# Holding the loads of two thirds back behind one-element copies, and moving the row sums and scalings of a third, in an attention kernel with a low-rank token mixer and an MLP

## Chip, cores and metric

One core of a Trainium2 chip runs the kernel. The metric is the device time of one execution in microseconds (us). Each of the five engines works through its own queue of instructions in program order: TensorE (PE, matmul), VectorE (DVE), ScalarE (ACT), GpSimd (POOL) and SyncE (SP). SP and POOL also issue DMAs, each into a queue of its own; 16 DMA engines serve both queues.

## What is computed

Attention with RMS-normalised queries and keys, then a mixer over the tokens and an MLP over the channels. B = 8 batches, 12 heads, 448 tokens, head size 64, so 768 channels; rank 32; hidden size 3072.

```python
q_n, k_n = rmsnorm(q, g_q), rmsnorm(k, g_k)
attn = softmax(q_n @ k_n.T / 8)
x = (attn @ v)                                # as [batch, 448, 768]
u = x + ((x.transpose(0, 2, 1) @ U) @ V).transpose(0, 2, 1)
out = u + relu(u @ w_ch1) @ w_ch2
```

## The kernel before, in words

A *third* is four heads of one batch: thirds 0 to 2 are batch 0, thirds 3 to 5 batch 1. A *pair* is two heads: pairs 0 to 5 are batch 0, pair 6 begins batch 1. Of each third, SP loads k and q (`load`, L209; side 0 is k, side 1 is q) and v (`load_v`, L220), 448 KB each. POOL or ACT squares k and q (`squares`, L234 and L236), DVE sums the squares by row (`reduce`, L242), ACT makes the reciprocal roots with a logarithm and an exponential (`rsqrt`, L247 and L248), and DVE scales into the bf16 tile `qkn` of a pair (`scale`, L256). There are two such tiles, used in turn. TensorE transposes a pair (`turn`, L267), DVE copies the result (`keep`, L274 and L278), TensorE makes the scores (`scores`, L300), ACT takes the exponentials (`expo`, L305), TensorE weighs v (`weigh`, L326), and DVE divides by the sums (`normalise`, L336 and L343).

For batch 0 the mixer goes in steps of 128 channels, `dc` = 0 to 5: `gather(dc)` (L401) multiplies by U, `gathered` copies, `spread(dc)` (L415, L417) multiplies by V, and `spreaded` (L422, L424) copies into `us[0]`, the MLP's input. The hidden layer is made in 24 blocks of 128. For batch 0, `first(i, ...)` (L889) makes blocks 0 to 3 channel by channel, as the channels arrive; `mlp(0)` makes blocks 4 to 23 (L541), and ACT or DVE evacuates them (L544, L546). The first weight w1 is loaded by POOL in four pieces (`load_w1`, L184): columns 0 to 511, 512 to 1023, 1024 to 2047 and 2048 to 3071. In hidden blocks these are 0 to 3, 4 to 7, 8 to 15 and 16 to 23. The second weight w2 comes in six pieces (`load_w2`, L192), the first behind `load_w1(3)`.

The order of the beginning is written out by hand: `head()` (L666 to L877) loads thirds 0 to 3 and the mixer's U and V (`load_mix`, L154 and L155), then goes through a list `plan` of steps. The steps fill the engines' queues in that order. The loads of thirds 4 and 5 stand in the plan, so they are issued on SP as soon as SP comes to them and their buffers are free. After `head()`, `weave` puts pieces of batch 1's attention between the blocks of `mlp(0)`, at due times that follow from weights: first `transposes(6)` (`turn(6)` and `keep(6)`), `load_w2(0, 0)` and the row sum of third 4's k, then what `attention(1)` lists. There POOL squares third 4's q and third 5's k and q, and casts the values of thirds 4 and 5, with the later pieces of w2 between them in its queue.

Some storage is borrowed: thirds 2 and 3 are loaded into `hT`, the place of the hidden layer; the squares of thirds 0 to 3 lie in `w2b`, the place of w2. A one-element copy on POOL after each scaling of the other thirds (`yield_port`, L573) makes POOL wait until DVE has scaled.

Of the kernel before, what the change touches and what calls it, by code (L numbers as in the profile page):

```python
# [10 lines left out]
BF16 = mybir.dt.bfloat16  # L11
# [6 lines left out]
def kernel(  # L18
# [13 lines left out]
    nc = tc.nc  # L32
# [27 lines left out]
    consts = ctx.enter_context(tc.tile_pool(name="consts", bufs=1))  # L60
# [135 lines left out]
    qks, vts, sqs, rstds, qkns, qkTs, scs, pts = {}, {}, {}, {}, {}, {}, {}, {}  # L196
# [29 lines left out]
    ALL = slice(0, HG)  # L226
# [42 lines left out]
    def keep(p, s, eng=None):  # L269

        if p not in qkTs:
            qkTs[p] = attn.tile([P, 2, S], BF16, tag="qkT", name="qkT")
        if s:
            nc.vector.tensor_scalar(qkTs[p][:, 1], pts[p][:, 1], gg, None, OP.mult)  # L274
        elif eng:
            nc.scalar.activation(qkTs[p][:, 0], pts[p][:, 0], AF.Copy)
        else:
            nc.vector.tensor_copy(qkTs[p][:, 0], pts[p][:, 0])  # L278

    def transposes(p):  # L280
        if p < NPE:
            turn(p)
            keep(p, 1)
            keep(p, 0)
        else:
            qkTs[p] = attn.tile([P, 2, S], BF16, tag="qkT", name="qkT")
            nc.sync.dma_start_transpose(qkTs[p].rearrange("d s (j p) -> d (s j) p", j=NJ),
                                        qkns[p].rearrange("p s j h d -> p (s j) (h d)"))
# [377 lines left out]
    def head():  # L666
# [33 lines left out]
            (squares, 1, ALL, (0,)),  # L700
            (gain,),
            (keep, 0, 0, 1),
            (heat, 13),
            (yield_port, 0, 1),
# [29 lines left out]
            (expo, 1, 0),  # L734
            (scores, 1, (1,)),
            (scores, 1, (2,)),
            (load, 4),
            (turn, 3),
            (expo, 1, 1),
            (scores, 1, (3,)),  # L740
# [19 lines left out]
            (setup_u, 1),  # L760
            (setup_u, 2),
            (cast_v, 1),
            (load_v, 4),
            (expo, 2, 2),
            (keep, 3, 0),
            (weigh, 0, 1),
# [16 lines left out]
            (keep, 4, 0),  # L783
            (normalise, 1, 0),
            (keep, 4, 1),
            (load, 5),
            (scores, 3, (2,)),
            (weigh, 1, 1),
            (scores, 3, (3,)),
# [10 lines left out]
            (gathered, 1, 1),  # L800
            (gathered, 0, 1),
            (scores, 4, (1,)),
            (load_v, 5),
            (scores, 4, (2,)),
            (spread, 1),
            (scale, 2, 1, (1,)),
            (turn, 5),
            (load_w1, 1),
            (normalise, 2, 0),
# [33 lines left out]
            (scores, 5, (3,)),  # L843
            (spread, 3),
            (spreaded, 2),
            (reduce, 3),
            (gather, 4),
            (expo, 5, 2),
            (squares, 4, ALL, (0,)),
# [4 lines left out]
            (spreaded, 3, 1),  # L854
            (weigh, 5, 0),
            (first, 1, (0, 1, 2, 3), True),
            (rsqrt, 3),
            (normalise, 5, 1),
            (normalise, 5, 0),
            (gather, 5),  # L860
            (scale, 3, 0),
            (gathered, 4, 1),
            (gathered, 5, 1),
            (spread, 4),
            (first, 0, (3,), False),
            (spreaded, 4, 1),
            (spread, 5),
            (first, 0, (4,), False),
            (spreaded, 5, 1),
            (first, 1, (4,), False),  # L870
            (first, 0, (5,), False),
            (first, 1, (5,), False),
            (scale, 3, 1),
            (load_w1, 3),
        ]
        for fn, *args in plan:
# [44 lines left out]
    with tc.manual_schedule():  # L921
        head()
        late = {7: (load_w2s, 1, 3), 8: (load_w2s, 3, 5), 9: (load_w2s, 5, 6)}
        for b in range(B):
            fill, total = mlp(b), volume(b)
            if b + 1 < B:
                later = []
                rest = [(4, lambda: (load_w2(0, 0), transposes(6), reduce(4, ALL, (0,))))] + attention(1, late, later)
                weave(fill, total * (0.72 if b in (4, 6, ) else FA[b % 2] if b else FA0), attention(b + 1) if b else rest)
                weave(fill, total * FM, mixing(b + 1))  # L930
                if b == 0:
                    weave(fill, total * FL, [(5 if w == .5 else 1, piece) for w, piece in later])
            for _ in fill:
                pass
# [30 lines left out]
```

## Time and profile before

| | |
|---|---|
| median of 4 runs | 576.16 us (575.08 to 576.36) |
| the profiled execution | 576.36 us |
| its span, first to last instruction | 574.6 us |
| PE, DVE, ACT, POOL busy | 98%, 67%, 49%, 14% of the span |
| `gather(5)` starts | 39.35 us |
| hidden block 4 starts (`mlp(0)`) | 41.90 us |
| the scores of pair 6 start | 46.30 us |
| hidden block 8 starts | 49.09 us |
| scalings of third 3 | 39.21 to 43.79 us |
| third 4: k, q, v issued | 22.21, 24.91, 26.26 us |
| third 5: k, q, v issued | 29.12, 33.76, 39.40 us |
| third 5: k, q, v landed | 56.2, 60.5, 63.8 us |
| third piece of w1 issued, landed | 29.21, 49.05 us |

Times are microseconds from the start of the span. In a row of a timeline the first number is the start and the second the duration; the square bracket gives the idle time of the engine before it and what ended that. In the chain of work that ended last, each row is a start, a length and what took it. A table by stretches gives the busy time of each engine with its number of instructions, the granted share of TensorE's clock, the busy share of the DMA engines (two queues can overlap on an engine, so it can pass 1) and the rate in GB/s. A row of a DMA queue gives packets, MB and the share of the 16 engines' time.

### The profile page before, as it was taken

What the parts mean: (1) busy time and instruction counts of PE and PEld (TensorE: products, weight loads), DVE (VectorE), ACT (ScalarE), POOL (GpSimd) and SP (SyncE); (2) the same over time, 40 slices, a digit from 0 to 9 for tenths busy, and PEclk for the clock granted to TensorE, in tenths of its full rate; (3) what the DMA queues carried; (4) which work ended last, traced back from release to release, by engine and by line L of the source; (5) the groups of instructions that cost most, each with busy time, mean ns of one, the idle gap of its engine ahead of it and who ended that gap; (6) DMA issues with size and microseconds to landing.
All of it is one profiled execution on the core that took longest, in us unless ns stands there. A gap on an engine that the chain in (4) does not pass through costs nothing.

```text
span 574.6 us, 11397 instructions
## 1 busy us (share of the span) xinstructions
PE 561.4 (98%) x4661; PEld 311.6 (54%) x4661; DVE 385.4 (67%) x755; ACT 280.2 (49%) x419; POOL 78.6 (14%) x124
## 2 busy tenths in 40 slices
PE   7998999999999999999999999999999999999997
PEld 5664555544565555544465555644456555654464
DVE  5985865799875788647776588747767486443442
ACT  5965652466621875076631777146661476302200
POOL 5662500100020000001020010000011000000010
PEclk9998999999999999999999999999999999999999
DMA  9999995733444565435534446455334541140021
GB/s 215 239 240 233 211 163 148 160 97 65 128 120 106 128 127 144 91 91 114 129 83 109 106 129 142 119 119 129 85 77 126 124 98 33 30 110 2 0 56 55
DMA packets 103648, 67.22 MB, mean 117 GB/s; under 512 B 54716, under 2 KB 102060, under 8 KB 103596
## 3 DMA queue, kind: packets, MB, share of 16 engines
q1 hardware_dynamic: 93988, 56.77, 41.8%
q0 software_dynamic: 9376, 9.44, 9.9%
q8 instruction: 36, 0.59, 0.4%
q10 hardware_dynamic: 232, 0.30, 0.1%
q14 instruction: 16, 0.13, 0.1%
HBM read 52.19 MB, written 11.01 MB: 110 GB/s over the span
## 4 chain that ended last, share of the span: by engine, by line
PE 90%; DMA 4%; DVE 2%; ACT 2%; POOL 1%; issue 0%; DVEq 0%; POOLq 0%
PE ph L541 37%; PE pb L466 11%; PE po L466 8%; PE pa L466 8%; PE pe L466 7%; PE sc L300 7%; PE bank L326 7%; DMA w1b<-in_moe_w_ch_dram 3%; PE pu L379 2%; PE bank L915 1%; ACT E L305 1%; PE o L326 1%; DMA u<-ring 1%; PE pm L365 1%; DVE qkn L256 1%; PE pt L267 1%
## 5 line engine op out<-in xcount | busy, mean ns | idle before, releaser
L541 PE MATMUL ph<-u,w1b 128*128 128x512 bf16 (+1 forms) x1128 | 234.2, 355 | 3.1 <-DMA w1b<-in_moe_w_ch_dram 2.2
L305 ACT ACTIVATE E<-sc 112x896 bf16<-112x896 f32 x184 | 158.3, 915 | 56.6 <-PE sc L300 56.5
L541 PEld LDWEIGHTS <-w1b 128*128 128x128 bf16 x1128 | 102.8, 98 | 111.1 <-issue 23.6
L466 PEld LDWEIGHTS <-hT 128*128 128x128 bf16 x1080 | 101.5, 98 | 71.1 <-issue 8.4
L544 ACT ACTIVATE hT<-ph 128x384 bf16<-128x384 f32 (+1 forms) x95 | 51.6, 543 | 133.9 <-PE ph L541 128.4
L546 DVE TENSOR_SCALAR hT<-ph 128x512 bf16<-128x512 f32 (+1 forms) x93 | 57.9, 622 | 51.0 <-PE ph L541 50.9
L326 PEld LDWEIGHTS <-E 112*128 112x128 bf16 x1472 | 58.9, 98 | 14.1 <-issue 1.1
L256 DVE TENSOR_TENSOR qkn<-qk,rstd 112x512 bf16<-112x512 f32 x84 | 54.3, 685 | 4.2 <-ACT rstd L248 2.7
L300 PE MATMUL sc<-qkT 64*128 64x448 bf16 x384 | 55.2, 356 | 1.9 <-ACT E L305 1.7
L242 DVE TENSOR_REDUCE rstd<-sq 112x16 f32<-112x1024 f32 x40 | 48.4, 1211 | 12.6 <-ACT sq L234 12.6
L326 PE MATMUL bank<-va,E 112*128 112x65 bf16 x1280 | 54.2, 194 | 0.0
L573 POOL COPY scratch<-qkn 1x1 bf16<-1x1 bf16 x44 | 10.5, 240 | 311.9 <-DVE qkn L256 311.9
L466 PE MATMUL po<-w2b,hT 128*128 128x384 bf16 x288 | 52.3, 326 | 0.1
L466 PE MATMUL pa<-w2b,hT 128*128 128x384 bf16 x264 | 49.2, 326 | 0.0
L466 PE MATMUL pb<-Tw,hT 128*128 128x384 bf16 x264 | 48.5, 326 | 0.0
L234 ACT ACTIVATE sq<-qk 112x1024 f32<-112x1024 f32 x36 | 38.2, 1061 | 6.7 <-DVE rstd L242 5.2
L381 DVE TENSOR_TENSOR ring<-pu,ring 128x768 bf16<-128x768 f32 (+3 forms) x36 | 31.0, 864 | 15.0 <-PE pu L379 14.2
L501 POOL TENSOR_TENSOR o<-o,ring 128x384 f32<-128x384 f32 x11 | 12.6, 1145 | 161.6 <-DVE o L500 161.6
L343 DVE TENSOR_TENSOR ring<-bank,rec 128x192 bf16<-128x192 f32 (+1 forms) x83 | 32.3, 389 | 1.9
L336 DVE RECIPROCAL rec<-bank 128x4 f32<-128x4 f32 x83 | 14.8, 179 | 26.8 <-PE bank L326 26.6
L300 PEld LDWEIGHTS <-qkT 64*128 64x128 bf16 x384 | 12.3, 94 | 33.7 <-issue 31.2
L481 ACT ACTIVATE pb<-pa 128x384 f32<-128x384 f32 x11 | 5.3, 481 | 50.2 <-PE pa L466 50.2
(111 smaller groups left out, 449.4 us busy)
## 6 DMA issues: line engine op xcount, KB each, us to landing
qk<-in_k_dram SPq DMA_DIRECT2D x21, 448.0 KB, 5.3
vt<-in_v_dram SPq DMA_DIRECT2D x20, 448.0 KB, 4.5
qk<-in_q_dram SPq DMA_DIRECT2D x19, 448.0 KB, 3.8
w2b<-in_moe_w_ch_dram POOLq DMA_DIRECT2D x6, 768.0 KB, 14.9
w1b<-in_moe_w_ch_dram POOLq DMA_DIRECT2D x2, 1536.0 KB, 18.3
out_dram<-o SPq DMA_DIRECT2D x15, 168.0 KB, 2.3
out_dram<-o SPq DMA_DIRECT2D x16, 144.0 KB, 2.0
out_dram<-o SPq DMA_DIRECT2D x15, 120.0 KB, 2.1
```

The lines of the kernel that those rows point to most:

```text
L234: nc.scalar.activation(sqs[t, s][:, hs], qks[t, s][:, hs], AF.Square)
L242: nc.vector.tensor_reduce(rstds[t][:, s, hs].rearrange("p h j -> p (h j)"), sqs[t, s][:, hs].rearrange("p h (j d) -> p (h j) d", d=D), AX, ...
L256: nc.vector.tensor_tensor(qkn[:, s].rearrange("p j h d -> p h j d"), qks[t, s][:, hp].rearrange("p h (j d) -> p h j d", d=D), rstd[:, s, h ...
L300: nc.tensor.matmul(sc[:, hh, 0:S], kT[pp, kc * SP:kc * SP + P], qT[pp, :], start=True, stop=True)
L305: nc.scalar.activation(E_of(p)[:, :, PAD + kc * S:PAD + (kc + 1) * S], scs.pop((p, kc))[0:SP, :, 0:S], AF.Exp, scale=float(D) ** 0.5)
L326: nc.tensor.matmul(o[:, n, :], E[:, hh, c:c + P], va[:, hl, kc, :], start=(kc == 0), stop=(kc == NJ - 1))
L343: nc.vector.tensor_tensor(ring[:, r0:r0 + t1 - t0, d0:d0 + D], o[:, t0:t1, 0:D], rec[:, t0:t1].rearrange("p c -> p c ()").to_broadcast([P, ...
L381: nc.vector.tensor_add(xv, pu[rows, 0:n, 0:HALF], xv)
L466: nc.tensor.matmul(ps, lhs[:, c, :], rhs[:, c, :], start=first and c == 0, stop=last and c == NC - 1, skip_group_check=again)
L541: nc.tensor.matmul(ph, w1b[:, dc, hc * P:(hc + 1) * P], u[:, dc, :], start=(dc == 0), stop=(dc == KD - 1))
L544: nc.scalar.activation(hT[:, hc, 0:n], ph, AF.Relu)
L546: nc.vector.tensor_relu(hT[:, hc, 0:n], ph)
```

## The change

A new step `gate(p)` copies one element of a scaled tile by a DMA on SP. The copy waits until the q side of pair p has been scaled, and since SP works in order, so do the loads behind it. `gate(5)` stands behind the last scaling of third 2, `gate(6)` behind the first two scalings of third 3. Third 4's k is loaded where it was. Its q is loaded behind `gate(5)`; its v, and k, q and v of third 5, behind `gate(6)`. The row sums of third 3 (`reduce(3)`) move behind the last normalisations of batch 0, and its `rsqrt(3)` and `scale(3, ...)` behind the last `spreaded`.

```diff
+    spots = consts.tile([1, 16], BF16, name="spots")
+
+    def gate(p):
+
+        nc.sync.dma_start(spots[:, p:p + 1], qkns[p][0:1, 1, 0, 0, 0:1])
...
-            (load, 4),
+            (load, 4, 1, (0,)),
...
-            (load_v, 4),
...
-            (load, 5),
...
-            (load_v, 5),
...
             (scale, 2, 1, (1,)),
+            (gate, 5),
+            (load, 4, 1, (1,)),
             (turn, 5),
...
-            (reduce, 3),
             (gather, 4),
...
             (first, 1, (0, 1, 2, 3), True),
-            (rsqrt, 3),
             (normalise, 5, 1),
             (normalise, 5, 0),
+            (reduce, 3, ALL, (0,)),
             (gather, 5),
-            (scale, 3, 0),
             (gathered, 4, 1),
             (gathered, 5, 1),
+            (reduce, 3, ALL, (1,)),
             (spread, 4),
             (first, 0, (3,), False),
             (spreaded, 4, 1),
             (spread, 5),
             (first, 0, (4,), False),
             (spreaded, 5, 1),
+            (rsqrt, 3),
+            (scale, 3, 0, (0,)),
+            (scale, 3, 0, (1,)),
+            (gate, 6),
+            (load_v, 4),
+            (load, 5),
+            (load_v, 5),
+            (scale, 3, 1),
             (first, 1, (4,), False),
             (first, 0, (5,), False),
             (first, 1, (5,), False),
-            (scale, 3, 1),
             (load_w1, 3),
```

## Prediction

> **What bounds the kernel now.** I read the chain of work that ended last first, then its rows around the change, then the granted clock in stretches, and last the DMA queues there.
>
> ```profile
> PE 90%; DMA 4%; DVE 2%; ACT 2%; POOL 1%; issue 0%; DVEq 0%; POOLq 0%
> ```
>
> ```profile
> 29.21 19.84 DMA w1b<-in_moe_w_ch_dram
> 49.05 0.05 issue
> 49.09 2.10 PE ph L541 x6
> ```
>
> TensorE carries 90% of the chain, and the change touches none of its work, so anything to win lies in the 4% of DMA. The chain of 26 to 60 us names it: the third piece of w1 (columns 1024 to 2047, issued by `load_w1(2)` at 29.21) lands at 49.05, and hidden block 8 starts at 49.09. TensorE was ready at 46.85 (the scores ahead end there), so 2.25 us are lost to waiting.
>
> ```profile
> 40.00:45.00 5.00, 5.00 (x37) 3.11 (x35) 3.79 (x4) 3.37 (x6) 3.76 (x4) 1.00 1.11 236
> 45.00:50.00 5.00, 2.75 (x21) 1.26 (x19) 2.34 (x4) 2.21 (x3) 1.89 (x1) 0.89 1.11 238
> 50.00:55.00 5.00, 4.77 (x29) 2.31 (x28) 2.64 (x5) 2.99 (x6) 0.00 (x0) 0.77 1.11 234
> 55.00:60.00 5.00, 5.00 (x52) 3.03 (x50) 4.54 (x11) 3.25 (x6) 3.86 (x5) 1.00 1.20 213
> ```
>
> These are the stretches (PE, PEld, DVE, ACT, POOL, then granted clock, DMA share, GB/s). The clock falls to 0.89 and 0.77 after the wait: (0.11 + 0.23) x 5 = 1.7 us more. The wait is thus worth up to 2.25 + 1.7 = 4 us. DMA share is over 1.1 throughout, so pieces compete: whatever is not moved before 49 lets the weights pass.
>
> ```profile
> q0 software_dynamic: 777, 1.56, 82.0%
> q1 hardware_dynamic: 793, 0.78, 28.5%
> ```
>
> That is the DMA view of 40 to 50 us: POOL's queue (q0, the weights) and SP's (q1, the loads of q, k and v). Both moved as many packets: on each of the 16 engines they take turns, one pair every 160/777 = 0.206 us, a 2 KB packet of weights for a 1 KB packet of loads. A packet of weights takes 0.82 x 160/777 = 0.169 us, and the two overlap by some 0.02. With the other queue empty a packet of weights would take 0.15 to 0.17 us, so each microsecond in which SP has nothing queued saves the weights 0.22 to 0.37 us.
>
> **The change, part by part.**
>
> *The two one-element copies.* The trace has none; the nearest rows are SP's shortest issue (0.31 us, third 6's k at 58.87) and the 0.5 KB gain loads (0.58 to 1.21 us to issue on ACT). I take 0.5 us on SP (0.3 to 1.2). SP issues nothing else between 39.97 and 58.87, so this hides; only the loads queued behind the copies wait. They also read the scaled tiles, which have two buffers: the next writer of the first one's buffer, `scale(3, 1)` at about 42.6, must wait for its end. It stands behind third 4's k, which POOL's squares saw land at 38.7, so there are 4 us of cover. The second one's buffer is next written at 54.7.
>
> *Third 4's q, moved from 24.91 to behind the first copy.* The copy waits for the last q scaling of third 2, done at 28.02. The load's first engine counts it at 31.6, its last at 44.39, so at 28.5 it still queues behind third 4's k. Cost and gain: nothing (0 to 0.3 us on engines that ran ahead).
>
> *Row sums of third 3 behind batch 0's last normalisation.* In the timeline around 38 us:
>
> ```profile
> 35.85 2.34 DVE L242 TENSOR_REDUCE rstd<-w2b 112x16 f32<-112x1024 f32 x2 [1.27 <-POOL w2b L236]
> ...
> 38.11 0.17 DVE L336 RECIPROCAL rec<-o 128x4 f32<-128x4 f32 x1
> ...
> 39.35 0.24 PE L401 MATMUL pm<-ring,Ub 128*32 128x128 bf16 x4 [1.05 <-DVE ring L343]
> ```
>
> Two row sums (2.34 us) stand ahead of the two normalisations that `gather(5)` needs. Without them these run when `weigh(5, 0)` ends (36.99): 0.17 + 0.42 us and small gaps give 37.7, so `gather(5)` starts when the matmuls ahead of it end (36.83 + 1.46 = 38.29) and not at 39.35: 1.06 us. TensorE then stands ready for block 8 at 46.85 - 1.06 = 45.8. That is no gain by itself: it is a longer wait, until the weights land.
>
> *The scalings of third 3.* Row sums 37.7 to 40.1, ln and exp (0.32 + 0.23, 0.58 with the gap in the trace) to 40.8. The four scalings took 4.58 us in the trace beside POOL's work (0.68 to 1.94 each, median 1.10). POOL's squares end at 40.6 and only its cast is beside them now, so I take 1.10 + 0.69: done at 42.6 (42.2 at 0.68 each, 43.9 at 1.94 + 1.10). `turn(6)` needs them at 44.83 - 1.06 = 43.8: 1.2 us of cover; past it the delay still vanishes in the wait for the weights. Behind them on DVE stand `keep(6)` (needed at 44.4) and two more scalings, with the same cover. ACT's queue behind the moved ln and exp holds the relu of `first`, not needed before the scores of pair 6.
>
> *The four loads behind the second copy* (v of third 4; k, q, v of third 5; issued before at 26.26, 29.12, 33.76, 39.40). They now issue from 42.6 + 0.5; the kernel's first load needs some 1.3 us to its first packets, so SP's queue fills again at 44.4 (44.0 to 45.7). From when is it empty? The landing counts of the trace (each engine counts its own part) say: twelve engines end third 4's q by 36.65, three at 40.0 to 40.9, one at 44.39. So twelve engines serve the weights alone for 7.7 us or more and save at least 7.7 x 0.22 = 1.7 us. The three save (44.4 - 40.3) x 0.22 to 0.37, 0.9 to 1.5 us. The last is empty for 0.4 us (0 to 1.7) and saves 0.1 (0 to 0.6).
>
> A DMA is done when its last engine is. Which one ends the third piece? It is counted from 46.02 to 49.05. The fourth piece's closing packets show four engines still sharing with SP, at 57.4, 57.5, 57.5 and 58.36; 48 pairs x 0.206 = 9.9 us earlier they ended the third, at 47.4 to 48.4, so were counted up to 48.7. The latest of the four must be SP's last one, since the piece of w2 that follows is 2.2 us later there than on any other. So the engine counted at 49.05 is one of the relieved twelve, and the lagging one becomes last: 48.7 - 0.1 = 48.6.
>
> Here a rule speaks against the change. The Trainium skill, DMA: Bandwidth & Descriptors, section "Why a DMA increments its semaphore by 16 and not by 1", says that a copy uses the largest number of engines, up to 16, that divides its slowest dimension. `load_mix` reads V as [4, 32, 448]: four engines carry its 224 KB, 56 KB each. The trace agrees: V's packets run at 13 to 18 us, the rate falls from 244 to about 196 GB/s, four landing counts belong to it, and four engines lag ever after. By the mean of the queues (SP had moved the 6.71 MB up to third 4's q at about 35 us) the weights would land near 46.3; by the slowest engine at 48.6. I take the slowest engine.
>
> A second rule would lower the stake: TensorE: Matmul & The Clock Gate, section "HAM oscillation — how this bites in real kernels", asks for idle gaps over some 3.4 us before the clock drops. The row shows it dropping after 2.25 us. By the rule the new gap (45.8 to 48.6, 2.8 us) costs no clock, by the row again 1.7 us. I take the row: no change there.
>
> **The sum.** 49.09 becomes 48.64: 0.45 us. Nothing later is pressed: on the lagging engine the held loads land as before (third 5's k 56.2, q 60.5), and after block 8 everything moves together. The profiled execution took 576.36 us (span 574.6), 0.2 above the median 576.16: 576.36 - 0.45 = 575.9, or 575.7 beside the median.
>
> **Rivals.**
>
> *The lag is absent or drained (full relief).* For: twelve engines are free from 36.65, and 1.7 us more of emptiness on the last one is within the bounds. Against: the 44.39 count. Then the weights land at 45.8 to 46.6, gain 2.9 us plus the clock's 1.7, less 0.3 because third 5's second squares now wait for q's landing at 60.5: 4.3 us, 571.9. With the clock dip kept, 573.6.
>
> *Third 5's k comes late (slower).* POOL squares it at 56.32, right as it lands; DVE's row sum of it starts at 61.73, in order. It may land until 61.73 - 1.89 - 0.1 = 59.7. From 44.4, v and k are 56 packets per engine, 56 x 0.206 = 11.5: 56.3. So the cover is 3 us; it is gone if the release comes after 47.5 or the weights take more than their half. Landing at 61.5, the sum blocks DVE (90% busy at 55 to 60) for 2.2 us, and with it the evacuations of the hidden blocks, for which TensorE waits: 575.7 + 2.2 = 577.9.
>
> **How the numbers follow.** Lagging engine decides: 0.50 (575.7, own range 574.9 to 576.4; 0.06 of it a gain over 0.2%). Full relief: 0.28. Late k: 0.15. Something unseen: 0.07, of it 0.05 slower. About 0.2%, 1.15 us, is what a measurement here can tell from no change. Faster 0.28 + 0.06 = 0.34; same 0.44 + 0.02 = 0.46; slower 0.20. The range runs from full relief, 571.8, to 577.4, short of the late k.
>
> **What would show it.** Right: block 8 starts at 48 to 49 with a wait of 2 us or more; `gather(5)` at 38.3; SP's queue empty on most engines at 37 to 44; clock dip kept. Wrong: block 8 at 46 with the clock at 1.00 (relief); a DVE wait for POOL's squares at 58 to 62 (late k); `turn(6)` after 45; or a wait of `scale(3, 1)` for a copy.

## The result, and the profile after

The changed kernel takes 575.08 us (median of 43 runs, 574.07 to 578.47); the kernel before, run again beside it, 576.5 us (median of 64). The ratio is 0.9975, 95% interval 0.9967 to 0.9983: 1.4 us or 0.25% faster. The forecast was 575.7 against 576.16, 0.45 us faster, "same" as the likeliest case. By the forecast's own line of 0.2% the change is just faster, the case that it gave 0.34.

The profiled execution took 574.89 us, with a span of 573.1. First its chain, by engine from the page, then the chain around the change: start, length, what took it.

```profile
PE 90%; DMA 7%; DVE 1%; POOL 1%; SPq 0%; issue 0%; ACT 0%; DVEq 0%; POOLq 0%
```

```profile
43.64 14.56 DMA qk<-in_k_dram
...
58.34 1.90 POOL sq L236
...
60.26 1.22 DVE rstd L242
61.48 0.36 DVE qkT L274
61.84 0.31 DVE qkT L278
62.15 0.14 issue
62.29 1.14 PE ph L547 x6
```

The DMA in the chain is another one: no longer the weights (29.21 to 49.05 before), but k of third 5, held back until 43.64 and landed at 58.20. Behind it stand POOL's squares, DVE's row sum, DVE's copies of pair 8's transposes, and a hidden block that waits for them at 62.29. TensorE's waits between 45 and 65 us, in total, number and longest:

```profile
PE ph L547 <- DMA w1b<-in_moe_w_ch_dram: 1.2, 1, 1.2
PE ph L547 <- DVE qkT L278: 1.2, 1, 1.2
```

The first was 2.2 us before; the second is new. The row of block 8:

```profile
47.59 1.15 PE L547 MATMUL ph<-u,w1b 128*128 128x384 bf16 x6 [1.25 <-DMA w1b<-in_moe_w_ch_dram]
```

The stretches show the same (PE, PEld, DVE, ACT, POOL, granted clock, DMA share, GB/s):

```profile
45.00:50.00 5.00, 3.75 (x31) 1.83 (x29) 3.08 (x7) 2.75 (x5) 1.89 (x1) 1.00 1.11 226
50.00:55.00 5.00, 4.75 (x44) 2.68 (x41) 4.36 (x9) 3.62 (x7) 0.18 (x1) 1.00 1.15 241
55.00:60.00 5.00, 5.00 (x57) 2.91 (x56) 3.76 (x10) 3.14 (x5) 1.66 (x1) 1.00 1.19 258
60.00:65.00 5.00, 3.77 (x37) 2.08 (x36) 3.57 (x8) 2.29 (x4) 5.00 (x7) 1.00 1.17 218
```

The clock stays at 1.00 where it was 0.89 and 0.77, and TensorE now idles at 60 to 65. In these two executions the sum runs so: block 8 starts at 47.59 and not at 49.09 (1.50 us); block 9 at 49.55 and not at 52.57, since the half clock is gone (3.02 by then); the late k takes 1.23 back; the first product with w2 starts at 76.81 and not at 78.42 (1.61), and the spans differ by 1.5.

The two DMA queues, again at 40 to 50 us:

```profile
q0 software_dynamic: 955, 1.92, 102.2%
q1 hardware_dynamic: 248, 0.25, 9.1%
```

The weights moved 955 packets instead of 777, SP's loads 248 instead of 793. Over 40 to 46 us SP's queue was empty on every engine (2 packets), and the weights' packets went out every 160 x 0.6/627 = 0.153 us per engine. The order on DVE at 38 us:

```profile
37.13 0.18 DVE L342 RECIPROCAL rec<-o 128x4 f32<-128x4 f32 x1 [1.94 <-PE o L332]
37.69 0.17 DVE L342 RECIPROCAL rec<-bank 128x4 f32<-128x4 f32 x1
38.24 2.34 DVE L242 TENSOR_REDUCE rstd<-w2b 112x16 f32<-112x1024 f32 x2
38.84 0.24 PE L407 MATMUL pm<-ring,Ub 128*32 128x128 bf16 x4
```

The row sums now follow the normalisations, and `gather(5)` starts without a wait.

Single executions differ much here. Third 1's v was counted on its slowest engine at 24.6 us in this execution and at 23.2 before, ahead of anything that the change moves; from there on this execution runs some 0.5 us later. Medians of many runs carry the verdicts below, and single profiles only the mechanism.

### The profile page after: what moved, and what is told of

It is laid out like the page before. It is cut to its first block, busy times and chain, and to the rows that moved or that the text cites. A ratio compares the mean times of both kernels' runs of the same rounds, so it can differ in the third digit from the quotient of the medians.

```text
span 573.1 us, 11403 instructions
## 1 busy us (share of the span) xinstructions
PE 559.3 (98%) x4661; PEld 310.4 (54%) x4661; DVE 383.7 (67%) x755; ACT 279.9 (49%) x419; POOL 77.9 (14%) x124
## 4 chain that ended last, share of the span: by engine, by line
PE 90%; DMA 7%; DVE 1%; POOL 1%; SPq 0%; issue 0%; ACT 0%; DVEq 0%; POOLq 0%
PE ph L547 36%; PE pb L472 11%; PE po L472 8%; PE pa L472 8%; PE pe L472 7%; PE bank L332 7%; PE sc L306 7%; DMA vt<-in_v_dram 3%; DMA qk<-in_k_dram 3%; PE pu L385 2%; PE o L332 1%; PE first L900 1%; DMA u<-ring 1%; PE pm L371 1%; DMA qk<-in_q_dram 1%
## 5 line engine op out<-in xcount | busy, mean ns | idle before, releaser
L311 ACT ACTIVATE E<-sc 112x896 bf16<-112x896 f32 x184 | 158.2, 915 | 55.9 <-PE sc L306 55.9
L349 DVE TENSOR_TENSOR ring<-bank,rec 128x192 bf16<-128x192 f32 (+1 forms) x83 | 32.3, 389 | 2.0
L306 PEld LDWEIGHTS <-qkT 64*128 64x128 bf16 x384 | 12.2, 94 | 34.0 <-issue 31.3
```

Of the source, the lines that this page charges most:

```text
L306: nc.tensor.matmul(sc[:, hh, 0:S], kT[pp, kc * SP:kc * SP + P], qT[pp, :], start=True, stop=True)
L311: nc.scalar.activation(E_of(p)[:, :, PAD + kc * S:PAD + (kc + 1) * S], scs.pop((p, kc))[0:SP, :, 0:S], AF.Exp, scale=float(D) ** 0.5)
L349: nc.vector.tensor_tensor(ring[:, r0:r0 + t1 - t0, d0:d0 + D], o[:, t0:t1, 0:D], rec[:, t0:t1].rearrange("p c -> p c ()").to_broadcast([P, ...
```

## The experiments

Theory 1: the gain is the earlier landing of the weights' third piece (with the half clock that it spares), less what third 5's late k takes back. Theory 2: the gain is the order on DVE, `gather(5)` 1 us earlier.

**The two halves of the change.** In `hold_only` the loads are held as in the change, and third 3 stays where it was:

```diff
-            (load, 4),
+            (load, 4, 1, (0,)),
...
-            (load_v, 4),
...
-            (load, 5),
...
-            (load_v, 5),
...
             (scale, 2, 1, (1,)),
+            (gate, 5),
+            (load, 4, 1, (1,)),
...
             (scale, 3, 0),
+            (gate, 6),
+            (load_v, 4),
+            (load, 5),
+            (load_v, 5),
```

> Only the loads are held (both one-element copies, q of third 4 behind the first, the other four loads behind the second); row sums, root and scalings of third 3 stay where they were in the kernel before. Theory 1 (the gain is the weights' third piece landing earlier, less what third 5's late k gives back): block 8 starts near 47.6 us with the clock at 1.00, and the time is within 0.5 us of the changed kernel, some 575.1 (ratio 0.9975). Since TensorE is ready only at 46.8 here, its wait is shorter, but the end is the same. Theory 2 (the moved row sums bring the gain, by starting gather(5) 1 us earlier): no gain, 576.5.

Measured: 575.42 us, ratio 0.9986 (0.9973 to 1.0). TensorE waited 0.3 us for the weights. The head of the profiled execution ran 3 us late, so block 8 at 50.40 says nothing. The gain leans to Theory 1, but its interval touches no change; what its runs say of the clock stands under `order_only`.

In `order_only` third 3's steps are moved as in the change, and all loads stay where they were, without copies:

```diff
-            (reduce, 3),
...
-            (rsqrt, 3),
...
+            (reduce, 3, ALL, (0,)),
             (gather, 5),
-            (scale, 3, 0),
...
+            (reduce, 3, ALL, (1,)),
...
+            (rsqrt, 3),
+            (scale, 3, 0, (0,)),
+            (scale, 3, 0, (1,)),
+            (scale, 3, 1),
...
-            (scale, 3, 1),
```

> Only the order on DVE and ACT is changed: row sums, root and scalings of third 3 late, all loads where they were, no copies. Theory 1: gather(5) starts 1 us earlier, but block 8 still waits for the weights until about 49.1 us and the clock dips, so the time is that of before, 576.5 (within 0.5). Theory 2: the gain of the changed kernel is here, 575.1.

Measured: 577.59 us, ratio 1.002 (1.0006 to 1.0033): slower. Theory 2 falls, and Theory 1's "no change" misses too. Its TensorE wait and stretches:

```profile
PE ph L547 <- DMA w1b<-in_moe_w_ch_dram: 3.7, 1, 3.7
```

```profile
45.00:50.00 5.00, 1.45 (x10) 0.47 (x8) 2.43 (x5) 1.81 (x3) 2.04 (x2) 1.00 1.11 248
50.00:55.00 5.00, 4.88 (x28) 2.33 (x28) 2.03 (x4) 2.53 (x5) 0.00 (x0) 0.66 1.11 227
```

TensorE is ready 0.4 us sooner than before (46.45 against 46.85), but in this execution the weights also came 1.0 us later (50.08 against 49.05), so most of the longer wait, 3.7 us against 2.2, is theirs. The half clock is as long as before: 0.34 x 5 = 1.7 us lost, here in one stretch and there in two.

Every run records its mean granted clock; a half clock of 3.4 us lowers that by 0.003. Runs at 0.997 or less: 94 of 149 of the kernel before, 7 of 44 of the changed one (one run more than the median counts; nine others stand at 0.998, with a median of 574.95), 20 of 22 here, and 2 of 22 of `hold_only`, where the kernel before, run beside it, had 51 of 75. So the held loads alone spare the half clock in most runs, and the earlier `gather(5)` alone does not. Why `order_only` is slower than before is only argued: it has the half clock more often, and twice in one run more often (0.995 or less: 8 of 22, against 20 of 149).

**The late k.** `k5_first` swaps two loads behind the second copy, `k5_later` two others:

```diff
# k5_first
             (gate, 6),
+            (load, 5, 1, (0,)),
             (load_v, 4),
-            (load, 5),
+            (load, 5, 1, (1,)),
# k5_later
             (load_v, 4),
-            (load, 5),
+            (load, 5, 1, (1,)),
+            (load, 5, 1, (0,)),
```

> The changed kernel with one swap: behind the second copy third 5's k is loaded ahead of third 4's v. Theory 1: k lands near 53 us and not at 58.2, POOL squares it at once, DVE's row sum of it no longer waits, and TensorE's wait of 1.2 us at 61 us goes: 573.9 (ratio 0.9955). Third 4's v lands near 58 us, when POOL's cast is about to need it. Rival (the wait at 61 us is made up later anyway, or goes over to the cast of v): as the changed kernel, 575.1.

Measured: 575.05 us, ratio 0.9985 (0.997 to 0.9999). In its profile POOL squares that k at 54.16 and not at 58.34, DVE's row sum waits for nothing, and TensorE waits 0.2 us there. That execution took 573.76 us, as Theory 1 said, but the median did not follow. Yet the wait that it takes away is no accident of one execution: the profiles of other kernels that load k in second place show 0.8 us (`hold_only`), 1.9 (`v_16_engines`) and 1.4 (`heat_after`); `touch_hold` alone has none. What takes its place in the usual execution, once k comes first, these runs do not show.

> The changed kernel with third 5's k one place later: v of third 4, q of third 5, k of third 5, v of third 5. If the wait of TensorE at 61 us is the price of a late k (rival of the prediction), k lands 3.5 us later, near 61.7, DVE's row sum waits some 5 us and not 1.5, TensorE some 4.8 and not 1.2, and the time is 2.5 to 3.6 us over the changed kernel: 577.6 to 578.7, slower than before. If the wait is made up later anyway, 575.1.

Measured: 581.08 us, ratio 1.0087 (1.0067 to 1.0107). Its waits at 55 to 72 us, and its stretches:

```profile
POOL sq L236 <- DMA qk<-in_k_dram: 9.2, 1, 9.2
...
DVE rstd L242 <- POOL sq L236: 5.5, 1, 5.5
PE ph L547 <- DVE qkT L278: 5.3, 1, 5.3
```

```profile
60.00:65.00 5.00, 0.87 (x6) 0.29 (x3) 0.85 (x1) 0.89 (x2) 2.78 (x2) 0.97 0.74 169
65.00:70.00 5.00, 3.83 (x27) 2.00 (x28) 2.74 (x9) 0.83 (x2) 5.00 (x7) 0.50 1.03 138
70.00:75.00 5.00, 5.00 (x40) 2.67 (x41) 4.47 (x9) 3.28 (x7) 0.84 (x2) 0.85 1.31 203
```

k waits on the DMA, POOL's squares on k, DVE's row sum on the squares, TensorE on DVE: 5.3 us. The half clock that follows ((0.03 + 0.50 + 0.15) x 5 = 3.4 us lost) was not in the expectation; with it the time exceeds the 577.6 to 578.7 expected, and all six runs have a half clock. The mechanism of the slower rival is real; the change stops one load short of it.

**The lagging engines.** `v_16_engines` and `v_16_before` load the mixer's V by four DMAs, in the changed kernel and in the kernel before:

```diff
-        nc.sync.dma_start(Vf, moe_V.rearrange("r s -> () r s").to_broadcast([4, rank, S]))
+        for i in range(4):
+            nc.sync.dma_start(Vf[i * rank:(i + 1) * rank], moe_V)
```

> The changed kernel with the mixer's V loaded by four DMAs of 32 rows each and not by one with a leading dimension of 4. If the four engines that carried V alone are those that lag (the prediction's reason for the small relief), the landing counts of third 4's q close up to within 3 us, the last near 38 us, and the third piece of w1 lands by 46.5 us: block 8 near 46.5 and up to 1 us less than the changed kernel, 574.1 to 575.1. If the lag has another cause, four counts of third 4's q are still late and nothing moves: 575.1. Three more issues on SP cost some 0.6 us each there, ahead of v of third 0.

Measured: 574.43 us, ratio 0.9967 (0.9954 to 0.998). The landing counts close up: third 3's v, in the changed kernel counted on twelve engines by 30.2 us and on the last four at 31.3, 31.5, 32.3 and 33.5, is now counted from 28.1 to 30.9. So V's load on four engines made those four lag. Third 4's q, though, is counted from 35.1 to 39.8, not within 3 us as expected, and a last count still comes late: third 4's k at 35.42, the other fifteen by 32.87; the third piece of w1 at 46.42, the others by 45.01. Whether that is one engine, and what holds it, the runs do not show. Block 8 starts at 46.63 without a wait. TensorE's waits at 40 to 70 us:

```profile
PE ph L548 <- DVE qkT L279: 1.9, 1, 1.9
```

The wait for the late k has grown from 1.2 to 1.9 us. Against the changed kernel the intervals overlap.

> The kernel before with V loaded by four DMAs over all 16 engines, and nothing else. If the four lagging engines matter only where SP's queue runs empty, nothing is won here: SP always has something queued, so the third piece of w1 still lands near 49 us and block 8 waits as before, 576.4 (within 0.5). If the lag itself is what delays the weights, block 8 starts 1 to 3 us earlier and the time is 573.5 to 575.5.

Measured: 576.23 us, ratio 0.9993 (0.998 to 1.0006); third 3's v is counted from 29.2 to 31.3, so the lag is gone here too, but the weights landed at 49.51 and TensorE waited 2.7 us. As expected, the lag matters only where SP's queue runs empty.

**The copies.** `touch_hold` holds the loads without a DMA. Before the load, DVE copies one element into its tile:

```diff
+        if p is not None:
+            nc.vector.tensor_copy(vt[0:1, 0, 0:1], qkns[p][0:1, 1, 0, 0, 0:1])
         nc.sync.dma_start(vt, ...)
...
-            (gate, 6),
-            (load_v, 4),
+            (load_v, 4, 6),
```

> The changed kernel with the loads held at the same two places, but without DMAs: in place of each copy DVE writes one element of the scaled tile into the tile that is to be loaded next, so that the load on SP waits for DVE. Theory A (the copy itself takes some 4 us from its issue to its packet, and the loads behind it wait in SP's queue for that): SP's first packets of third 4's v come 1 to 1.5 us after its issue, near 44 us and not 46.8; third 5's k lands near 55.5 us and not 58.2, so TensorE's wait of 1.2 us at 61 us goes; but the weights have the DMA engines to themselves for 3 us less, and block 8 starts up to 1 us later, near 48.3, perhaps with the clock dip: between 574.0 and 576.5. Theory B (any load that SP issues while POOL's queue keeps the engines busy needs 4 us to its first packet): first packets again 4 us after the issue, and the time of the changed kernel, 575.1.

Measured: 574.88 us, ratio 0.9975 (0.9959 to 0.9992). The issues on SP, of the changed kernel and then of this one:

```profile
42.55 0.58 SPq L284 DMA_DIRECT2D spots<-qkn  x1
43.22 0.33 SPq L220 DMA_DIRECT2D vt<-in_v_dram  x1
```

```profile
43.18 0.31 SPq L224 DMA_DIRECT2D vt<-in_v_dram  x1
```

The DMA queues of this run, from 44.1 to 46.6 us and from 46.6 to 46.8:

```profile
q0 software_dynamic: 229, 0.46, 100.8%
```

```profile
q0 software_dynamic: 18, 0.04, 97.2%
q1 hardware_dynamic: 6, 0.01, 11.1%
```

In the changed kernel the copy's packet went out at 46.81, 4.3 us after its issue, and v's first ones at 46.73, 3.5 us after theirs. Without a copy v's first packets came at 46.65, again 3.5 us after the issue. Theory A falls: the copies cost next to nothing. What is slow is the load itself, issued into SP's nearly empty queue while POOL's keeps the engines busy: of the seven other runs that hold the loads, six also show 3.5 us, and `touch_k5_first_v_16` (below) 2.6. The kernel's first load, issued at 0.74 with no other load under way, has its first packet at 1.78, and in the kernel before third 6's q, issued at 85.80 with POOL's queue empty, at 86.85. That is close to Theory B; why it takes 3.5 us the runs do not show.

**The clock alone.** `heat_before` and `heat_after` put matmuls on zeros into the wait:

```diff
+            if b == 0 and hc == 8:
+                heat(18)    # 9 in the changed kernel
             ph = ps_mm.tile([P, n], FP32, tag="mm")
```

> The kernel before with 18 matmuls on zeros (240 columns each, into the unused part of their PSUM bank, as the beginning has them) in front of hidden block 8, that is in TensorE's wait for the weights: some 2.0 us of work in a wait of 2.25 us. Nothing is read from them and the output is the same. If the changed kernel's gain is mainly that fewer executions see the half clock after the wait (executions at a mean clock of 0.998 or more had a median of 575.0 to 575.6 us before and 575.0 after, those below 576.9 and 576.4), the half clock goes and the time is near 575.1 with the weights landing as late as ever. If the gain is the weights' earlier landing, this stays at 576.4.

Measured: 575.72 us, ratio 0.9994 (0.9975 to 1.0013). One run of 12 had the half clock, against 9 of 23 of the kernel before beside it, and the profile has 1.00 throughout. Where so few had it there was little to win: (39 - 8)% of 1.7 us is 0.5 us, and the means differ by 0.5 (576.15 and 575.65). But the interval holds both no gain and the changed kernel's ratio: the half clock is spared, and what that alone is worth stays open.

> The changed kernel with 9 such matmuls (1.0 us) in front of hidden block 8, whose wait is 1.25 us in the trace. One execution in six saw the half clock in the changed kernel; without it the median moves by 0.3 us at most: 574.8 to 575.1. If the matmuls delay block 8 where the weights are early, up to 1 us more.

Measured: 575.68 us, ratio 0.9991 (0.9975 to 1.0008), no better than the changed kernel: in its profile the weights land at 46.21, before the matmuls on zeros end, so these have become the delay.

**Together.** `k5_first_v_16` joins k first and V on 16 engines; `touch_k5_first_v_16` has DVE's element in place of the copies as well.

> The changed kernel with both edits: third 5's k ahead of third 4's v behind the second copy, and V loaded by all 16 engines. By the theory that the two waits are separate (weights at 47.5 us, third 5's k at 58.2 us), both go: block 8 starts near 46.6 us, DVE's row sum at 60 us waits for nothing, and the time is 1.2 to 1.9 us below V on 16 engines alone: 572.5 to 573.3 (ratio 0.993 to 0.9945). Rival (something else is late next and takes the place of the wait for k): as V on 16 engines alone, 574.4.

> As the one before, with DVE's one-element writes in place of the two copies. Theory A: SP's queue fills again 3 us earlier; third 5's k lands near 50 us, with no use, and the weights lose those 3 us alone, 0.7 us of landing: block 8 at 46.6 to 47.3; the time is the same as with the copies or up to 0.7 us more, 572.5 to 574. Theory B: the same as with the copies.

Measured: 574.04 us, ratio 0.9957 (0.9932 to 0.9982), and 573.16 us, ratio 0.9939 (0.9919 to 0.9959). In the first one's profile block 8 starts at 47.05 with nothing to wait for, and the row sum of k does not wait. Its gain fell short of the 572.5 to 573.3 expected. The second, inside its expected range, is the fastest version here, and the only one whose interval lies clear of the changed kernel's. Its one profiled execution took 576.48 us with a half clock at 70 us, so it does not show what the median does.

## Why the prediction was right in sign and too small

That the time came out so near the forecast is luck in part. Of its four signs of being right, SP's empty queue came, and `gather(5)` without a wait, at 38.84 in an execution that ran 0.5 us late. Block 8 started at 47.59 and not at 48 to 49, after a wait of 1.2 us and not 2, and the clock stayed at 1.00. The relief was larger than forecast, and a late k, which the sum had at nothing and the rivals at 0.15, took part of it back.

- *What bounds the kernel* held: the wait for the third piece of w1, and the half clock behind it.
- *The two copies* took 0.70 and 0.58 us on SP (0.5 estimated), and nobody waited for their end.
- *Third 4's q*: first counted at 36.1 and not at 31.6, more than the 0.3 us allowed, but its squares still started when the tile for them was free (46.87).
- *Row sums* and *scalings of third 3*: `gather(5)` without a wait, as said. The first two scalings were done by 42.55 (42.6 estimated), and `turn(6)` did not wait. That the earlier `gather(5)` is "no gain by itself" was right but too kind: `order_only` is 0.2% slower.
- *The four loads behind the second copy* is where the sum was mis-sized: "the kernel's first load needs some 1.3 us to its first packets, so SP's queue fills again at 44.4 (44.0 to 45.7)". The first packets came at 46.7, some 4.2 us after the release and outside these bounds. The 1.3 us were read where no other queue was busy (the trace has 1.04 there). From this term two others follow. The slowest engine ended third 4's q at 40.7 in this execution, so SP's queue was empty there for 6 us and not for 0.4; the weights came at 47.54 and not at 48.6. And third 5's k came at 58.20, not "as before" at 56.2 (nor at the 56.3 of the rival, whose own sum, 44.4 + 11.5, gives 55.9).
- The count of 44.39 was itself one execution's. In the nine profiles with held loads third 4's q ended on the slowest engine at anything from 39.8 to 46.3. In `touch_hold` it ended at 44.37, and there the forecast came true: the weights landed at 48.52, TensorE waited 2.3 us, and the clock fell.
- *The lagging engine*: that V's load makes four engines lag was right (`v_16_engines`), and one engine was still last; its relief was mis-sized. That V alone makes the last one late was not: with V on 16 engines one still ended the weights 1.4 us after the rest.
- *The clock*: "by the row again 1.7 us. I take the row: no change there" failed. In the profile the clock stays at 1.00. The row gave one execution; over many the share of runs with a half clock grows with the wait that the profile shows for block 8: 2 of 22 at 0.3 us (`hold_only`), 16% at 1.2, 63% at 2.2, 15 of 22 at 2.7 (`v_16_before`), 91% at 3.7; `touch_hold`, 6 of 20 at 2.3, stands out. The length does not decide alone: the profile of `touch_k5_first_v_16` has a half clock after a wait of 1.68 us, that of `v_16_engines` none after 1.88. So neither the row nor the rule of 3.4 us beside it tells a single execution.
- What the clock is worth: in the mean the changed kernel gains 576.40 - 575.31 = 1.1 us. Runs of the kernel before with the half clock are 1.7 us longer than those without, and 63 - 16 = 47% of 1.7 is 0.8 us of it. Runs without it differ by 0.25 us in the mean (575.31 and 575.06). `hold_only` points the same way against the kernel before beside it: 575.14 and 575.16 without a half clock, so its gain lies in the share. That split is only argued: the runs without a half clock may be those in which the weights came early, the changed kernel's 44 runs and the 149 were not taken side by side, and `heat_before` did not decide it.
- *Rivals*: full relief did not come, but its spared half clock did. The late k came in part; `k5_later` showed mechanism and price.

What was won from the weights and the clock, 3.0 us in the two profiles, was given back by 1.2 us at 61 us in that execution; in the median, taking the late k away (`k5_first`, 575.05) won nothing more.

## What to carry to other kernels

Holding loads back helps only from the moment the other queue is truly alone on the last DMA engine: count on the slowest engine and on the first packets, not on the issue. Order the held loads by who needs them first, and work out the margin of each. A gain upstream of a wait can cost: TensorE waits longer, and its clock falls more often.

## What the runs showed of the hardware

- A load issued on SP while POOL's queue kept the engines busy and SP's was empty, or nearly, took 3.5 us to its first packets in eight profiles and 2.6 in a ninth, and 1.04 us at the kernel's start, with no other load under way; a one-element copy took 4.3 us (changed kernel).
- A load whose leading dimension was 4 made four engines lag: third 3's v, behind it, ended on them at 32.1 to 35.1 us in the kernel before, on the other twelve by 30.7. With the same data in four loads of 32 rows it ended on all sixteen by 31.3 (`v_16_before`).
- A half clock came after waits of TensorE in a share of the executions, from 16% where the profile's wait was 1.2 us to 91% where it was 3.7. It lasted 3.4 us, in `k5_later` 6.8 us.
